# Splitting the last chunk of a start-up weight load over two DMA queues, and three more dummy matmuls beside it

## Chip, cores, metric

One core of one Trainium2 chip. The metric is the device time of one execution in microseconds (us). Beside it each run has a *span*: first to last instruction of the program, as the profiler records them.

## The reference

A conditioned transformer block on 2048 tokens of width 512: `mod = silu(c) @ w_mod` gives six vectors of 512; a layer norm is scaled and shifted by two of them, followed by attention with 32 query heads over the last 512 cached keys of 8 key heads, an output projection, a gated residual, and a second normalised and gated MLP.

```python
mod = (_silu(c) @ w_mod).reshape(c.shape[0], 6, 1, -1)
sa, ca, ga, sb, cb, gb = (mod[:, 0], mod[:, 1], mod[:, 2], mod[:, 3], mod[:, 4], mod[:, 5])
h = _layernorm(x, axis=-1) * (1 + ca) + sa
x = x + ga * _A_ref(h, A_k_cache, A_v_cache, A_wq, A_wo)
h = _layernorm(x, axis=-1) * (1 + cb) + sb
x = x + gb * _B_ref(h, B_w1, B_w2)
```

The first two slices of `w_mod` (for `sa` and `ca`) are needed before anything else, so their load stands at the very start.

## The kernel before

The loads at the start are issued from the sync engine (SP) and the scalar engine (ACT). Each chunk of `wm01` is 128 rows of 2 KB.

```python
    for i in range(2):
        dma(x_sb[:, 2 * i:2 * i + 2, :], ..., f"xa{i}", ..., eng=ACT if i else SP)
    dma(c_row[:, :], ...)
    for i in range(DC):                       # DC = 4
        load_wm01(i, (ACT, SP)[i % 2])
    for i, eng in enumerate((SP, SP)):
        dma(wq_sb[:, 2 * i:2 * i + 2, 0:QA * Dh], ...)   # first query weights
    load_k(0); load_wq(2, 2); load_v(0)
```

TensorE meanwhile runs dummy matmuls, then 32 products of one column (eight per chunk), transposes, two more dummies and the rest of the transposes:

```python
    def warm(n, gate=(), bk=7):               # n dummies of 512 columns into a spare bank
        for i in range(n):
            mm(bank[bk], ones[:, :], ones[:, 0:1].to_broadcast([P, QB]), True, True, ...)
    ...
    fs = mod_cols_mm(0, QBK)                  # 4 chunks x 2 slices x 4 columns
    for f in fs:
        f()
    ln_tposes(0, TB[0])
    mod_cols_evac(0, QBK)
    ... # cut
    ln_tposes(1, TB[0])
    warm(2, bk=1)
    ln_norm(2)
    mod_half(0, 0, DVE)
    mod_half(0, 2, ACT)
    ln_tposes(2, TB[1])
    ln_tposes(3, TB[1])
```

The kernel holds a second, general program as a fallback for odd values. A flag decides near the end, and here the fallback never runs. On TensorE it stands *after* the normal ending, so TensorE's last act is a jump over it:

```python
                if name == "pe":
                    with e.If(v == 128):
                        last_part()
                    with e.Else():
                        rerun()               # emits the general program; never runs here
```

## Time and profile before

| | before |
|---|---|
| time, 3 runs at first | 560.16 us (560.13 to 560.22) |
| span of the profiled run | 559.0 us (that run's time: 560.87) |
| TensorE busy | 553.9 us, 99% of the span |
| last chunk of the modulation weights lands | 8.82 us |
| first score matmul | 11.65 us |

TensorE is the bound from 11.65 us on.

### The profile page before, as it was taken

What the parts mean: (1) busy time and instruction counts of PE and PEld (TensorE: products, weight loads), DVE (VectorE), ACT (ScalarE), POOL (GpSimd) and SP (SyncE); (2) the same over time, 40 slices, a digit from 0 to 9 for tenths busy, and PEclk for the clock granted to TensorE, in tenths of its full rate; (3) what the DMA queues carried; (4) which work ended last, traced back from release to release, by engine and by line L of the source; (5) the groups of instructions that cost most, each with busy time, mean ns of one, the idle gap of its engine ahead of it and who ended that gap; (6) DMA issues with size and microseconds to landing.
All of it is one profiled execution on the core that took longest, in us unless ns stands there. A gap on an engine that the chain in (4) does not pass through costs nothing.

```text
span 559.0 us, 9759 instructions
## 1 busy us (share of the span) xinstructions
PE 553.9 (99%) x4139; PEld 316.6 (57%) x4139; DVE 254.9 (46%) x556; ACT 349.4 (63%) x455; POOL 52.7 (9%) x50
## 2 busy tenths in 40 slices
PE   8999999999999999999999999999999999999997
PEld 4665555555555555555555555555555554444444
DVE  5555555553546544335445443333354438322134
ACT  5986666666666666666666666666666644432500
POOL 2000022004400000033000000332000000000000
PEclk9999999999999999999999999999999999999999
DMA  9999763422224244353353312121123110200001
GB/s 234 296 196 185 136 166 42 114 43 73 38 41 74 39 84 106 61 130 58 96 95 57 76 40 39 39 38 38 39 39 76 39 29 0 50 28 21 21 29 48
DMA packets 113356, 42.66 MB, mean 76 GB/s; under 512 B 93976, under 2 KB 112152, under 8 KB 113304
## 3 DMA queue, kind: packets, MB, share of 16 engines
q1 hardware_dynamic: 112584, 41.08, 35.5%
q10 hardware_dynamic: 720, 0.89, 0.5%
q8 instruction: 33, 0.54, 0.4%
q14 instruction: 19, 0.16, 0.1%
HBM read 18.35 MB, written 2.10 MB: 37 GB/s over the span
## 4 chain that ended last, share of the span: by engine, by line
PE 98%; DMA 1%; SPq 0%; DVE 0%; issue 0%
PE psS L1374 29%; PE psO L1374 27%; PE psQ L1374 23%; PE psW L1374 20%; DMA wmw<-in_w_mod_dram 1%; SPq L1303 0%; PE psS L1377 0%; PE psO L1377 0%; DVE PT L1752 0%; DVE PT L1754 0%; PE psW L1377 0%
## 5 line engine op out<-in xcount | busy, mean ns | idle before, releaser
L1498 ACT ACTIVATE PT<-psS 128x1024 bf16<-128x1024 f32 x254 | 260.4, 1027 | 127.0 <-PE psS L1374 126.9
L1374 PE MATMUL psS<-qT,kT 128*128 128x512 bf16 (+1 forms) x516 | 151.8, 377 | 0.1
L1374 PEld LDWEIGHTS psO<-v,PT 128*128 128x128 bf16 x2048 | 126.6, 98 | 30.2
L1374 PE MATMUL psO<-v,PT 128*128 128x129 bf16 x2048 | 137.0, 220 | 0.0
L1374 PE MATMUL psW<-wo,oT 128*128 128x512 bf16 x512 | 130.6, 379 | 0.0
L1374 PE MATMUL psQ<-hT,wq 128*128 128x512 bf16 (+1 forms) x508 | 129.6, 377 | 0.0
L1508 DVE RECIPROCAL rinv<-psO 128x4 f32<-128x4 f32 x128 | 23.3, 182 | 225.3 <-PE psO L1374 225.3
L1509 DVE TENSOR_TENSOR o<-psO,rinv 128x512 bf16<-128x512 f32 x128 | 88.5, 691 | 4.7 <-DVE rinv L1508 0.3
L1374 PEld LDWEIGHTS psS<-qT,kT 128*128 128x128 bf16 x516 | 50.0, 98 | 58.7 <-issue 0.4
L1374 PEld LDWEIGHTS psQ<-hT,wq 128*128 128x128 bf16 x508 | 49.7, 98 | 59.0 <-ACT hT L1641 0.2
L1490 ACT ACTIVATE qT<-psQ 128x512 bf16<-128x512 f32 x125 | 73.9, 591 | 0.0
L1741 ACT ACTIVATE wq<-psS 128x512 bf16<-128x512 f32 x56 | 33.4, 597 | 49.1 <-PE psS L1374 49.1
L1374 PEld LDWEIGHTS psW<-wo,oT 128*128 128x128 bf16 x512 | 45.0, 98 | 32.9 <-DVE acc L1531 1.2
L1531 DVE TENSOR_TENSOR acc<-psW,acc 128x512 f32<-128x512 f32 x48 | 33.2, 691 | 6.7 <-PE psW L1374 6.7
L1374 PE MATMUL psO<-wmw,wq 128*128 128x512 bf16 (+1 forms) x168 | 32.9, 352 | 0.0
L1534 POOL TENSOR_TENSOR acc<-acc,gaf 128x512 f32<-128x512 f32 x12 | 15.6, 1301 | 146.9 <-DVE acc L1531 139.8
L1390 POOL TENSOR_TENSOR rstd<-rstd,cst 128x4 f32<-128x4 f32 x7 | 7.2, 1027 | 216.6 <-DVE rstd L1389 216.6
L1752 DVE TENSOR_TENSOR PT<-psO,gbf 128x512 f32<-128x512 f32 (+1 forms) x12 | 7.5, 624 | 40.4 <-PE psO L1374 40.4
L1374 PE MATMUL psS<-h2T,wmw 128*128 128x512 bf16 x112 | 25.3, 379 | 0.0
L1374 PEld LDWEIGHTS psO<-wmw,wq 128*128 128x128 bf16 x168 | 15.4, 98 | 16.5
L1374 PE MATMUL psS<-hT,wmw 128*128 128x512 bf16 x112 | 24.5, 379 | 0.0
L1384 DVE BATCH_NORM_STATS2 st<-x 128x6 f32<-128x512 bf16 x31 | 21.1, 680 | 3.7 <-DMA x<-in_A_x_dram 3.7
(93 smaller groups left out, 197.1 us busy)
## 6 DMA issues: line engine op xcount, KB each, us to landing
wo<-in_A_wo_dram SPq DMA_DIRECT2D x4, 1024.0 KB, 5.9
wq<-in_A_wq_dram SPq DMA_DIRECT2D x7, 512.0 KB, 4.5
wmw<-in_B_w_dram SPq DMA_DIRECT2D x14, 256.0 KB, 3.1
wmw<-in_w_mod_dram SPq DMA_DIRECT2D x4, 512.0 KB, 5.0
oT<-o SPq DMA_TRANSPOSE x128, 2.4
out_dram<-PT SPq DMA_DIRECT2D x15, 128.0 KB, 1.7
x<-in_A_x_dram SPq DMA_DIRECT2D x3, 512.0 KB, 4.3
v<-in_A_v_cache_dram SPq DMA_DIRECT2D x8, 128.0 KB, 4.5
```

The source lines that it names most:

```text
L1374: kb.op(PE, lambda e: e.matmul(out_ap, lhsT, rhs, start=start, stop=stop), reads=reads, group_writes=[R_b[k] for k in bk], signal=signal)
L1384: kb.op(DVE, lambda e: e.bn_stats(st[:, t, :], x_sb[:, t, :]), reads=[R_x[t]], writes=[R_st[t]])
L1390: kb.op(POOL, lambda e: e.tensor_tensor(rstd[:, sl], rstd[:, sl], cst[:, 0:1].to_broadcast([P, hi - lo]), op=ALU.pow), reads=R_rstd[sl] + ...
L1490: kb.op(ACT, lambda e: e.activation(qT[u % NQT][:, :], bank[bk], ACTF.Copy), reads=[R_b[bk]], writes=[R_qT[u % NQT]])
L1498: kb.op(ACT, lambda e: e.activation(PT[u % NPT][:, pr * 2:pr * 2 + 2, :], s_ps[pr][:, :, :], ACTF.Exp, scale=scale), reads=[R_b[pr * 2], R ...
L1508: kb.op(DVE, lambda e: e.reciprocal(rinv[:, u, :], o_ps[:, :, P]), reads=[R_b[5], R_b[6]], writes=[R_rinv])
L1509: kb.op(DVE, lambda e: e.tensor_tensor(o_sb[u % NOS][:, :, :], o_ps[:, :, 0:P], rinv[:, u, :].unsqueeze(2).to_broadcast([P, TPB, P]), op=A ...
L1531: kb.op(DVE, lambda e: e.tensor_tensor(acc[:, tl, :], bank[WBK], acc[:, tl, :], op=ALU.add), reads=[R_b[WBK], R_acc[tl]], writes=[R_acc[tl]])
L1534: kb.op(eng, lambda e: e.tensor_tensor(acc[:, tl, :], acc[:, tl, :], gaf[:, :], op=ALU.mult), reads=[R_acc[tl], R_ga], writes=[R_acc[tl]])
L1741: kb.op(ACT, lambda e: e.activation(h1T[b % 2][:, fc, :], bank[bk], ACTF.Relu), reads=[R_b[bk]], writes=[R_h1[b % 2][fc]], pre=all_events( ...
L1752: kb.op(DVE, lambda e: e.tensor_tensor(yt[i][:, c0:c1], bank[bk][:, c0:c1], gbf[:, c0:c1], op=ALU.mult), reads=[R_b[bk], R_gb], writes=[R_ ...
```

## The change

Its intent: let the last chunk come over both queues at once, and keep TensorE at work in the gaps so that its clock stays up.

```diff
-    R_wmc = RL("wmc", DC)
+    R_wmc = RL("wmc", DC + 1)
@@
     def load_wm01(i, eng=None):
-        dma(wm01[:, i, :], wm01v[:, i, :], f"wmc{i}", writes=[R_wmc[i]], eng=eng)
+        if i < DC - 1:
+            dma(wm01[:, i, :], wm01v[:, i, :], f"wmc{i}", writes=[R_wmc[i]], eng=eng)
+        else:
+            for sl, eng in enumerate((ACT, SP)):
+                dma(wm01[:, i, sl * D:(sl + 1) * D], wm01v[:, i, sl * D:(sl + 1) * D], f"wmc{i + sl}", writes=[R_wmc[i + sl]], eng=eng)
 
     def wm_res(sl, cc):
-        return R_wmc[cc] if sl < 2 else R_wm[sl]
+        return R_wmc[cc + (sl if cc == DC - 1 else 0)] if sl < 2 else R_wm[sl]
@@
-    for f in fs:
+    for i, f in enumerate(fs):
         f()
+        if i in (7, 23):
+            warm(1, bk=6)
@@
     ln_tposes(1, TB[0])
-    warm(2, bk=1)
+    warm(3, bk=1)
```

## The prediction

> **What bounds the kernel now.** I read the page first: busy shares, then the chain that ended last.
>
> ```profile
> PE 553.9 (99%) x4139; PEld 316.6 (57%) x4139; DVE 254.9 (46%) x556; ACT 349.4 (63%) x455; POOL 52.7 (9%) x50
> ...
> PE 98%; DMA 1%; SPq 0%; DVE 0%; issue 0%
> ```
>
> TensorE (PE) is busy for 99% of a span of 559.0 us, and 98% of the chain lies on it. The only other entry is 1% of DMA, the load of the first modulation weights, `wmw<-in_w_mod_dram`. Whatever the change does must therefore happen in the start, before PE runs without a break. So I asked for the chain by time over the first 12 us (columns: start us, length us, what).
>
> ```profile
> 2.05 6.77 DMA wmw<-in_w_mod_dram
> 8.82 0.05 issue
> 8.87 0.35 PE psQ L1374 x8
> 9.22 0.47 PE psS L1377 x8
> 9.69 0.43 PE psS L1374 x2
> 10.12 0.11 PE psO L1377 x2
> ...
> 10.57 0.52 PE psQ L1374 x4
> 11.09 0.44 PE psO L1374 x4
> 11.52 0.13 issue
> 11.65 0.38 PE psS L1374 x2
> ```
>
> The reader sees: the last chunk of the modulation weights, issued at 2.05 us, lands at 8.82; its eight one-column products (psQ), eight transposes, two dummies (psS L1374 x2), more transposes, then the first query products follow on PE with no real gap. From 11.65 on PE stays on the chain to the end. A delay or gain before that point reaches the end nearly one to one.
>
> The timeline of PE shows how the chunks come (start, length, what, idle before it and what ended it).
>
> ```profile
> 7.37 0.34 PE L1374 MATMUL psQ<-sc_bf,wmw 128*128 128x1 bf16 x8
> 8.11 0.55 PE L1374 MATMUL psQ<-sc_bf,wmw 128*128 128x1 bf16 x16 [0.40 <-DMA wmw<-in_w_mod_dram]
> 8.87 0.35 PE L1374 MATMUL psQ<-sc_bf,wmw 128*128 128x1 bf16 x8 [0.21 <-DMA wmw<-in_w_mod_dram]
> 9.08 0.61 PE L1377 MATMUL psS<-ident,xn 128*128 128x128 bf16 x8
> ```
>
> Two idle gaps, 0.40 and 0.21 us, each ended by a chunk's landing. The semaphore records of the trace give the landings: chunk 0 (ACT queue) 5.45, chunk 1 (SP) 8.06, chunk 2 (ACT) 8.24, chunk 3 (SP) 8.82. Each counts sixteen engine completions, and the last is an outlier: for chunk 3 fifteen are in by 7.93 and the sixteenth comes 0.89 us later. One slow DMA engine sets the time. The packet records show that engine alone from 7.5 us: a 2 KB packet about every 80 ns, first alternating between the two queues, then, after ACT's last packet ends at 7.84, the eight packets of chunk 3 back to back until 8.48; the semaphore follows 0.34 us later.
>
> VectorE (DVE) and ScalarE at the same place:
>
> ```profile
> 8.08 0.73 DVE L1395 TENSOR_SCALAR xn<-x,mv,rstd 128x512 bf16<-128x512 bf16 x2
> 9.26 0.17 DVE L1440 TENSOR_TENSOR modc<-psQ,m 128x8 f32<-128x8 f32 x1 [0.45 <-PE psQ L1374]
> 9.34 0.40 DVE L1395 TENSOR_SCALAR xn<-x,mv,rstd 128x512 bf16<-128x512 bf16 x1
> 9.73 0.73 DVE L1639 TENSOR_SCALAR hT<-psS,modc 128x256 bf16<-128x256 bf16 x2
> ```
>
> DVE idles 0.45 us before it copies out the products (modc), so at most about 0.45 us is to be won by an earlier landing: after that DVE's own normalisation, which ends at 8.81, is the bound.
>
> **What the Trainium skill says.** "DMA: Bandwidth & Descriptors", section "Issuing engines are not separate DMA queues": transfers issued from the scalar and the sync engine run on the same 16 DMA engines and interleave; a second issuer saves only sequencer time. The trace agrees: the slow engine alternates between the two queues at the same 80 ns a packet. The same page, "Queues, rings and completion order", says that each DMA engine goes round-robin between the queues it has work for, packet by packet; I use that to order the halves. "TensorE: Matmul & The Clock Gate", "Wait — 56ns, not 53.3ns?", gives 426.7 ns between 512-column matmuls cold and 215.7 warm. The trace agrees: the dummies start 427 ns apart until about 6.9 us, then the two at 9.53 and 9.74 are 216 ns apart. Its section "What's actually happening" puts the return to the cold clock after an idle window of about 3.4 us; the idle gaps here are 0.40 and 0.21 us, and no cold spacing returns in this trace.
>
> **The change, part by part.**
>
> (a) *The split.* Chunk 3 was one 256 KB DMA on the SP queue, 128 rows of 2 KB; it becomes two of 128 KB, rows of 1 KB, one on each queue. One issue more on ACT: about 0.45 us (its two wmw issues take 0.94), at 2.17, ahead of the table load. That load would end near 3.9 instead of 3.48, and ACT has nothing to do before x lands at 4.93: hidden. The queues were balanced before: ACT carried half of x and chunks 0 and 2, SP the other half and chunks 1 and 3, 768 KB each. After, ACT has 896 KB and SP 640 KB, with SP's next load, the first query weights (512 B rows), moving up behind its half. On the slow engine: the bytes are the same, but by the packet records' medians sixteen 1 KB packets take 16 x 46 = 0.74 us where eight of 2 KB take 8 x 84 = 0.67: +0.07. Round-robin then: SP's last packet of chunk 1 ends at 7.67, ACT has two of chunk 2 left (0.17). SP's half gets two in between, six of each side alternate to about 8.47, and ACT's last two share with two query-weight packets of 27 ns: 8.47 + 2 x 46 + 2 x 27 ns = 8.62, plus the 0.34 = 8.96. Against 8.82 that is +0.14; with better overlap of the small packets it is nearer +0.05. I take +0.10 us, on the path.
>
> (b) *Dummies after products 8 and 24.* Two 512-column matmuls on bank 6, 216 ns each at the warm rate. The first lies in the 0.40 us gap. The second follows chunk 2's products, whose last starts at 8.50, so it holds the array until about 8.74, and chunk 3 can start at 8.87 as before. Bank 6 has no reader yet, so no wait is added. Cost 0 as long as chunk 3 does not come earlier; else up to 0.2.
>
> (c) *Third dummy between the transposes.* Before, the two stream from 9.53 to 9.96, and the next transposes start exactly then: the dummies, not the data (the normalised tile was ready at 9.75), set that start. A third moves them to 10.18 and the first query product from 10.41 to 10.62. The four products of that group started at 10.41, 10.52, 10.62 and 10.80; the last waited for ScalarE's hT, ready at 10.75. Now, at 0.11 us each: 10.62, 10.73, 10.84, 10.95. So 0.15 of the 0.216 us stays on the path, through the copy of the query (11.12) to the first scores (11.65).
>
> Sum: +0.10 + 0 + 0.15 = +0.25 us; from 560.16 that is 560.4.
>
> **The rivals.**
>
> *R1: the split does bring the chunk earlier.* For it: fifteen of sixteen engines were done by 7.93, so another mix of packets may spare the slow engine its stall (one of its 2 KB packets may be the one of 746 ns at 6.07, which I cannot prove). Against: total bytes and engines are the same, and 2 KB and 1 KB rows differ little. Worth at most 0.45 us by DVE's idle time, less 0.15 for (c) and up to 0.2 for the second dummy: 559.7 to 560.1.
>
> *R2: the dummies mend the clock.* For it: that is evidently their aim, and nothing but them keeps PE busy between chunks. Against: the spacing is already 216 ns at 9.53 and stays there, and three runs agree within 0.09 us; there is nothing left to mend. Then (b) and (c) are worth zero or less. The opposite, a relapse to the cold clock for one window, would cost about half of 3.4 us, an estimate from the page's window: 561.9. I give it 2%.
>
> *R3: the load is hidden anyway*, because the landing is replaced by another wait at the same place: the query weights, landed at 9.22 and 9.74, are needed only from 10.41, and the keys, landed at 10.30, from 11.65. They have 0.6 us or more of slack, so I do not expect them to show. Then the result would be (c) alone: 560.3.
>
> **Range and chances.** Everything moves inside a stretch of 3 us out of 560; 2% would be 11.2 us, which no step here can reach. My middle is 560.35, between the sum and R1's pull downward. The range runs from R1's best, with the dummies hidden, to the sum with a slow engine delayed a further 0.5 us: 559.6 to 560.9. Faster by over 2%: 0.005; within 2%: 0.99; slower: 0.005.
>
> **What would show it right or wrong.** In the changed profile: (a) a third wmw issue on the ACT queue near 2.2 us, and the last eight products starting at 8.9 to 9.0 instead of 8.87; at 8.6 or earlier R1 holds. (b) One psO matmul in each gap, the idle gaps shorter by about 0.2 us and the products no later. (c) Three psS dummies 216 ns apart, the next transposes 0.2 us later relative to the last product, the first scores about 0.25 us later than 11.65. From there on the two traces should run parallel to the end. The prediction fails if the slow DMA engine is gone or slower still, or if the spacing falls back to 427 ns anywhere after 7 us.

## The result, and the profile after

| | time, us | span, us | time minus span, mean |
|---|---|---|---|
| before, same series, 6 runs | 560.23 (560.13 to 560.43) | 559.0 in the profiled run | 1.9 in the profiled run |
| change, 6 runs | 561.82 (561.33 to 562.19) | 558.3 to 559.0, mean 558.6 | 3.17 |

The ratio is 1.0027 (95% interval 1.0014 to 1.0040). I had said 560.35, between 559.6 and 560.9; the result lies outside. By the 2% class it is "same", but the six runs do not overlap with before's.

Now the profile. The page of the change opens with the same span to the tenth, and with almost the same busy times:

```profile
span 559.0 us, 9766 instructions
## 1 busy us (share of the span) xinstructions
PE 554.3 (99%) x4142; PEld 316.5 (57%) x4142; DVE 255.1 (46%) x556; ACT 349.6 (63%) x455; POOL 52.7 (9%) x50
```

Three more matmuls, three more weight loads, one more DMA issue: seven instructions, and no microsecond lost inside the span. The chain by time over the first 12 us (start, length, what):

```profile
2.20 6.44 DMA wmw<-in_w_mod_dram
8.64 0.05 issue
8.68 0.35 PE psQ L1378 x8
9.04 0.47 PE psS L1381 x8
9.51 0.65 PE psS L1378 x3
10.15 0.11 PE psO L1381 x2
...
10.64 0.56 ACT hT L1647
11.20 0.28 ACT qT L1627
11.49 0.14 issue
11.62 0.38 PE psS L1378 x2
```

In this trace the last half chunk, now ACT's, lands at 8.64 (before: 8.82). The three dummies hold TensorE for 0.65 us instead of 0.43, and the first scores start at 11.62 (before: 11.65). The dummies in the gaps are where they were meant to be:

```profile
7.12 0.35 PE L1378 MATMUL psQ<-sc_bf,wmw 128*128 128x1 bf16 x8
7.33 0.38 PE L1378 MATMUL psO<-ones 128*128 128x512 bf16 x1
7.77 0.59 PE L1378 MATMUL psQ<-sc_bf,wmw 128*128 128x1 bf16 x16
8.22 0.38 PE L1378 MATMUL psO<-ones 128*128 128x512 bf16 x1
8.68 0.35 PE L1378 MATMUL psQ<-sc_bf,wmw 128*128 128x1 bf16 x8
```

The extra issue on ACT pushes the table load to 2.69, as expected, and ACT still waits for x afterwards:

```profile
1.23 1.42 ACTq L1303 DMA_DIRECT2D wmw<-in_w_mod_dram  x3
2.69 1.28 ACT L1587 ACT_TABLE_LOAD   x1 [2.69 <-issue]
...
4.87 0.63 ACT L1589 ACTIVATE xn<-x 128x512 bf16<-128x512 bf16 x1 [0.68 <-DMA x<-in_A_x_dram]
```

From there the two traces run parallel: the last matmul ends at 555.80 before and at 555.77 after. So the loss is outside the span. The trace also holds what happens there, as semaphore updates without instructions. After the last instruction come a first group of nine updates of semaphore 2, then about 250 semaphores cleared in five ranges of some 50 side by side, then a second group of nine:

| us from the span's start | before | change |
|---|---|---|
| first group | 559.20 to 559.74 | 559.24 to 559.78 |
| semaphores 3 to 53 cleared, last | 560.31 | 560.35 |
| other four ranges cleared, last | 560.18 | 560.23 |
| second group | 560.53 to 560.89 | **561.96 to 562.32** |
| that run's time | 560.87 | 562.14 |

Up to the last clear the two agree within 0.05 us. Then the change waits 1.6 us where before waits 0.2, and the second group's end is the run's time within 0.2 us in both.

What does it wait for? The DMA view of the last microseconds of the change:

```profile
q8 instruction: 2, 0.03, 2.1%
q14 instruction: 1, 0.01, 0.4%
```

These are fetches of instructions. Queue 8 moves packets of 16,384 bytes, 33 in all: 0.54 MB, about the size of TensorE's 8284 recorded instructions (4142 matmuls and as many weight loads) at 64 bytes. The last one lands at 560.52 in the change, and the second group starts 1.44 us later. The Trainium skill, "Runtime: NRT & Kernel Launch", section "Instruction fetch mechanics", says that an engine's instructions are streamed in blocks of 16 KiB (256 instructions), that crossing a boundary is "mostly hidden", and that a taken branch breaks the prefetch. The same page, "The ~15µs preamble/postamble breakdown", lists a barrier, 51 semaphore resets per engine and another barrier after the kernel. The updates above look like that.

**Theory P (placement).** TensorE jumps over the fallback at the very end and fetches the block of its target. The closing code follows. The change lengthens TensorE's program by six instructions: TensorE's built program has 914,240 bytes instead of 913,856, which is 6 x 64. So the closing code lies 384 bytes further on, and a block boundary now falls ahead of the second barrier. TensorE gets there before the next block can be used.
**Theory A:** ScalarE's extra instruction, or the extra semaphore, lengthens the closing part.
**Theory C:** the start itself is slower in runs without a profile (a lost clock, another order of the DMAs).

### The profile page after: what moved, and what is told of

The parts are those of the page before. It is cut to its first block, busy times and chain, and to the rows that moved or that the text cites. A ratio compares the mean times of both kernels' runs of the same rounds, so it can differ in the third digit from the quotient of the medians. Undisturbed runs are those within 1.5% of the kernel's fastest.

```text
span 559.0 us, 9766 instructions
## 1 busy us (share of the span) xinstructions
PE 554.3 (99%) x4142; PEld 316.5 (57%) x4142; DVE 255.1 (46%) x556; ACT 349.6 (63%) x455; POOL 52.7 (9%) x50
## 4 chain that ended last, share of the span: by engine, by line
PE 98%; DMA 1%; ACTq 0%; ACT 0%; DVE 0%; issue 0%
PE psS L1378 29%; PE psO L1378 27%; PE psQ L1378 22%; PE psW L1378 20%; DMA wmw<-in_w_mod_dram 1%; ACTq L1303 0%; ACT hT L1647 0%; PE psS L1381 0%; PE psO L1381 0%; DVE PT L1758 0%; DVE PT L1760 0%; ACT qT L1627 0%; PE psW L1381 0%
```

## The experiments

For most of them I lengthen TensorE's program in the fallback, which never runs. Every executed instruction stays the same and only addresses move:

```diff
+        for _ in range(K // 2):      # a matmul is a weight load and a matmul: two instructions
+            PE.ops.append((lambda e: e.matmul(ps[0][0:1, 0:1], ones[:, 0:1], ones[:, 0:1], start=True, stop=True), [], []))
         SP.ops.append((lambda e: e.nop(), final_waits, []))     # end of the general program
```

I first tried no-operations there, but the build drops them. All sixteen runs below gave the reference's result. Below, *gap* is the time from the end of the first group to the start of the second in the profiled run, and *tail* the mean of time minus span. Before has gap 0.80 and tail 1.77 to 1.85.

### before_pad6: K = 6, before's instructions at the change's addresses

> The kernel before plus six TensorE instructions in the fallback program, which never runs: every executed instruction is the same, only TensorE's closing code lies 384 bytes further on, as in the change. Theory P (the time is lost after the last instruction, because TensorE's closing code now crosses a boundary of its instruction fetch): time 561.3 to 562.0, span as before, last closing semaphore update about 1.4 us later. Theory A (ScalarE's extra DMA issue or the extra semaphore lengthens the closing part) and theory C (the start itself became slower in runs without a profile): 560.2, same as before.

561.13 us (560.94 to 561.35) against 560.14 for before in the same rounds; gap 1.86, tail 2.92; the spans are *shorter* than before's if anything (558.0 to 558.5). Not one executed instruction differs, and 1.1 us are lost after the last. The loss is a matter of placement. (I had said 561.3 to 562.0: the direction is right, the size a little short.)

### change_pad250: the change with K = 250, so 256 instructions over before

> The change plus 250 TensorE instructions in the fallback program that never runs, so that TensorE's program is 256 instructions (16384 bytes) longer than before's and its closing code lies at the same place in a 16 KB block. Theory P: 560.0 to 560.4, the loss of 1.6 us gone. Theories A and C: 561.8 as the change.

560.50 us (559.93 to 561.17), gap 0.80, tail 1.80. With the closing code moved on to 256 instructions over before's, its old place within a 16 KB block by theory P, the loss of the change is gone. (The time is a little above my 560.0 to 560.4.) Theory A falls: ScalarE's instruction and the semaphore are still there.

### split_only: the diff without the three dummies

```diff
# against the change
-    for i, f in enumerate(fs):
+    for f in fs:
         f()
-        if i in (7, 23):
-            warm(1, bk=6)
-    warm(3, bk=1)
+    warm(2, bk=1)
```

> The split without any of the three dummies. TensorE's program has before's length, ScalarE's is one instruction longer, one semaphore more. Theory P: 559.9 to 560.3 (landing 0.2 us earlier as in the change's trace, no third dummy). Theory A: 561.3 to 562.0. Theory C with the DMA order at fault: 561.5 or more.

Gap 0.80, tail 1.81, so on the closing part P is right and A wrong once more. But the time is 561.61 (559.99 to 562.17), and this time it is lost *inside* the span: three of six runs have spans of 560.3 to 560.4 and a mean granted clock of 0.996 to 0.997. The profiled run is one of them. Two stretches of it (start:end and length in us; then the busy time and number of instructions of TensorE, its weight loads, VectorE, ScalarE and GpSimd; then the granted clock, the DMA share and GB/s):

```profile
6.43:9.85 3.42, 2.30 (x45) 1.59 (x43) 2.43 (x11) 1.39 (x4) 2.05 (x4) 1.00 1.26 195
9.85:13.26 3.41, 3.41 (x22) 2.32 (x20) 2.00 (x6) 1.96 (x4) 0.00 (x0) 0.50 1.19 287
```

For one window of 3.41 us the clock is at half, right after a window with little TensorE work. The timeline shows the cost:

```profile
9.19 0.35 PE L1378 MATMUL psQ<-sc_bf,wmw 128*128 128x1 bf16 x8 [0.37 <-DMA wmw<-in_w_mod_dram]
...
11.54 1.06 PE L1378 MATMUL psQ<-hT,wq 128*128 128x256 bf16 x4
12.40 1.03 PE L1378 MATMUL psO<-hT,wq 128*128 128x256 bf16 x4
13.25 0.61 PE L1378 MATMUL psS<-qT,kT 128*128 128x256 bf16 x4
```

Four query products take 1.03 us instead of 0.60, and the first scores start at 13.25. So Theory C is wrong for the change, whose traced starts are sound, but it names a real thing: this is what the dummies are for.

### dummies_only: the three dummies without the split

```diff
# against before; R_wmc, load_wm01 and wm_res stay as they were
+        if i in (7, 23):
+            warm(1, bk=6)
-    warm(2, bk=1)
+    warm(3, bk=1)
```

> The three dummies without the split. TensorE's program is six instructions longer, ScalarE's as before. Theory P: 561.5 to 562.0 (the closing 1.4 us plus about 0.15 for the third dummy), span up by about 0.15. Theory A: 560.4. Theory C: between 560.2 and 560.6.

561.63 us (561.20 to 562.26), gap 2.13, tail 3.05, mean span 558.6. ScalarE's program is as before, TensorE's is six instructions longer, and the loss is there: P.

### before_pad2, before_pad4, before_pad30, before_pad64: step or slope

> Two TensorE instructions more in the fallback that never runs (128 bytes). Theory P: the loss is a step, not a slope: either the closing gap between the two groups of closing updates is 0.8 us (time 560.1) or about 2 us (time 561.3), nothing between; with two instructions I expect 0.8 and 560.1. Rival S (each added instruction costs the same, 1.2 us over six): 560.5.

> Four more (256 bytes). Theory P: again 0.8 or about 2 us, whichever side of the step it is on. Rival S: 560.9.

> Thirty more (1920 bytes): the boundary then falls in the middle of TensorE's 51 closing semaphore clears. Theory P: its clears come in two bursts, split by the fetch, and the closing gap is 2.0 to 2.6 us (time 561.3 to 561.9). Rival S: 565 or more.

> Sixty-four more (4096 bytes): TensorE's program then ends beyond the boundary, so its closing code lies whole in the block that its last jump fetches anyway. Theory P: closing gap 0.8 us or less, time 560.1, in spite of ten times the added instructions. Rival S: 570 or more, or at least no less than with thirty.

Times 560.25, 561.22, 560.32 and 560.26 us against 560.18; tails 1.81, 2.91, 1.84, 1.83. It is a step, and the rival with a cost per instruction is dead: 64 instructions more cost nothing. With four the second group starts on time (gap 0.80) but needs 0.89 us instead of 0.36: the wait is now inside it, which my "0.8 or about 2 us, nothing between" had not foreseen. (One of its four runs, 564.2, also lost the clock window.) My own expectation for thirty was wrong: no two bursts, no loss, gap 0.86. The losing placements are a window, and I did not know its width.

### third_pad254, gaps_pad252, split_gaps_pad252, change_pad250b: the parts inside the span

All are padded to 256 instructions over before, so that the closing code is out of the way.

```diff
# third_pad254:       before, with warm(3, bk=1) for warm(2, bk=1);            K = 254
# gaps_pad252:        before, with the "if i in (7, 23): warm(1, bk=6)";       K = 252
# split_gaps_pad252:  the change, with warm(2, bk=1) for warm(3, bk=1);        K = 252
# change_pad250b:     the change;                                              K = 250
```

> Only the third dummy between the transposes, with TensorE's program padded to 256 instructions over before's, so that the closing code lies as before. My step (c): span 0.15 us over before's, time 560.3. If the third dummy is hidden: 560.1 to 560.2. Closing gap 0.8 us.

> Only the two dummies in the gaps between the chunks' products, padded likewise. My step (b): no cost, 560.1 to 560.2, and no run with the clock window lost (granted clock 0.996 or 0.997, 562.1). If the second dummy delays the last chunk's products: 560.3 to 560.4.

> The split and the two gap dummies, without the third, padded likewise: the best version by the parts if the split gains the 0.1 to 0.2 us that the change's trace shows at the landing. Then 559.9 to 560.2 and no lost clock window. If the split brings nothing in the mean: 560.2 to 560.6, as wide as the change with padding.

> The padded change a second time, in the same rounds as its parts: 560.2 to 560.7 (560.50 the first time), closing gap 0.8 us. Its difference to split_gaps_pad252 is the third dummy: 0.15 us by my step (c).

| kernel | time, us | runs that lost the clock window | mean span of the others | gap |
|---|---|---|---|---|
| before, same rounds | 560.35 (559.98 to 561.82) | 3 of 11 | 558.41 | – |
| third dummy only | 560.53 (560.30 to 561.81) | 1 of 6 | 558.72 | 0.80 |
| two gap dummies only | 560.33 (560.20 to 560.79) | 0 of 5 | 558.56 | 0.80 |
| split and gap dummies | 560.26 (560.22 to 560.48) | 0 of 5 | 558.50 | 0.80 |
| change, padded | 560.51 (560.19 to 560.84) | 0 of 6 | 558.63 | 0.80 |

The spans of one kernel scatter by 0.2 to 0.7 us, so differences of 0.1 between these means are not resolved. (The medians of the third dummy alone and of the gap dummies alone lie 0.1 to 0.2 us above what I had expected.) The third dummy alone can be had more sharply, from the traces. Where the last chunk's landing is the bound, I take the time from its first product to the first scores. Without the third dummy that is 2.78 (before: 8.87 to 11.65) and 2.79 us (before_pad18 below); with it 2.93 (third_pad254) and 2.94 (the change: 8.68 to 11.62). The two chains, first before_pad18, then third_pad254:

```profile
8.14 0.35 PE psQ L1376 x8
8.49 0.47 PE psS L1379 x8
8.97 0.43 PE psS L1376 x2
...
10.93 0.60 PE psS L1376 x4
```

```profile
8.68 0.35 PE psQ L1376 x8
9.03 0.47 PE psS L1379 x8
9.49 0.65 PE psS L1376 x3
...
10.63 0.56 ACT hT L1643
11.19 0.28 ACT qT L1625
11.48 0.14 issue
11.61 0.49 PE psS L1376 x3
```

So the third dummy costs 0.15 us on the path. The second gap dummy can hold the products: in gaps_pad252 chunk 3 had landed at 7.85, yet its products start only at 8.28, behind the dummy at 8.06.

```profile
7.66 0.54 PE L1376 MATMUL psQ<-sc_bf,wmw 128*128 128x1 bf16 x16
8.06 0.38 PE L1376 MATMUL psO<-ones 128*128 128x512 bf16 x1
8.28 0.34 PE L1376 MATMUL psQ<-sc_bf,wmw 128*128 128x1 bf16 x8
```

(The first dummy delays the products of chunks 1 and 2 there in the same way.) But the 0.22 us of the second do not reach the scores, because with so early a landing another chain is the bound: x, its statistics and its normalisation on VectorE, for which the transposes wait. In before_pad12, where chunk 3 lands at 7.52, the chain shows it:

```profile
0.79 3.76 DMA x<-in_A_x_dram
...
7.97 0.33 DVE xn L1397
8.30 0.05 issue
8.35 0.72 PE psS L1379 x8
...
11.03 0.60 PE psS L1376 x4
```

VectorE's second normalisation ends at 8.62 there, the transposes that read it start at 8.67, and the first scores follow 2.41 us after its end. The same 2.41 or 2.42 us are found with K = 2, 4, 6, 24 and 64, and in gaps_pad252 with its dummies (8.82 to 11.24). So in six of ten traces of before's own start the last chunk was not the bound at all, and a still earlier landing would have gained nothing.

The split's own effect stays open. Over ten traces of before's own start (before and its padded versions) the last chunk lands anywhere from 7.52 to 8.82 us; over five traces with the split the last half lands from 7.96 to 9.14. A tenth of a microsecond cannot be seen in that, and it would count only in the runs that the landing bounds. The best candidate, the split with the gap dummies, is at 0.9993 of before (95% interval 0.9979 to 1.0008): steadier in these runs, not shown to be faster.

### before_pad8, before_pad12, before_pad18, before_pad24: where does the wait sit?

> Eight TensorE instructions in the fallback. If the loss is a wait at the place where TensorE's closing code crosses into its next instruction block (theory P), two instructions earlier than with six: closing gap about 2 us, time 561.2. If only exactly four to six instructions lose (something else that the placement touches), gap 0.8 and 560.2.

> Twelve. Theory P: about 2 us again; if the crossing has by then moved into TensorE's semaphore clears, one of the five ranges of clears ends 1 to 1.4 us later than the other four, which names TensorE's range.

> Eighteen. Theory P in its first form (the crossing moves through the clears): one range of clears in two bursts, gap about 2 us. As thirty showed no loss, the other form is that the window of losing placements has ended: gap 0.8 to 0.9.

> Twenty-four, next to thirty, which lost nothing. Gap 0.8 to 0.9 and time 560.2 if the window ended before; about 2 us if it ends between 24 and 30.

Two runs each. Times 562.93, 563.05, 560.14 and 560.30 us against 560.10. Put in order of K, with the other placements, the wait walks backwards through the closing sequence (us from each span's start; "fetch" is the landing of the last 16,384-byte packet on queue 8):

| K | first group ends | fetch lands | clears of 3 to 53 end | second group | time minus span | the wait sits |
|---|---|---|---|---|---|---|
| 0 | 559.74 | 560.44 | 560.31 | 560.53 to 560.89 | 1.77 to 1.85 | nowhere |
| 2 | 559.13 | 559.61 | 559.71 | 559.93 to 560.29 | 1.81 | nowhere |
| 4 | 559.34 | 559.64 | 559.91 | 560.14 to 561.03 | 2.91 | within the second group |
| 6 | 559.24 | 559.55 | 559.82 | 561.10 to 561.46 | 2.92 | before the second group |
| 8 | 561.13 | 561.78 | 563.57 | 563.80 to 564.15 | 3.58 | before these clears (the other ranges ended by 561.53) |
| 12 | 562.00 | 559.90 | 562.57 | 562.80 to 563.15 | 1.75 | before the first group, inside the span |
| 18 | 559.05 | 559.68 | 559.63 | 559.85 to 560.21 | 1.84 | nowhere |
| 24 | 559.36 | 559.86 | 559.94 | 560.16 to 560.52 | 1.90 | nowhere |

With K = 8 the one range 3 to 53 is cleared 2 us after the other four, so that range belongs to the engine that waits (I had expected this for K = 12). With K = 12 the wait has moved in front of the program's last barrier, whose instruction on TensorE starts at 561.35 instead of about 558.3, and so it shows in the span:

```profile
core 0: 561.4 us, clock 0.997
```

(The 0.997 is the half clock while TensorE stands still at the end; this start lost no window. The profiled run with K = 8 did lose one, hence its late times; its second run, 561.89 with a span of 558.3, did not.) In these losing traces the engine goes on 1.4 to 1.6 us after the fetch has landed: 1.44 in the change, 1.55 with K = 6, 1.46 with K = 8, 1.45 with K = 12. The fetch itself keeps its schedule: in all eighteen traces, losing or not, it starts 2.12 to 2.16 us after the fetch before it has landed. What K moves is the instruction that needs the block. The size of the loss also follows the fetch: it took 1.22 us in the change and 0.95 with K = 6, most of the difference between their gaps (2.18 and 1.86). And at K = 18 nothing waits any more; by theory P the boundary then lies ahead of the place that the jump goes to, and all of the closing code is in that block. That last step is inferred from the pattern; the walk is measured.

One more rival can be settled from the traces: in each of them the granted clock falls to half at some point after the last matmul. With K = 18 it falls at 557.39, before the closing part, and nothing is lost; with K = 6 it falls only at 560.46, when the wait (559.82 to 561.10) is already under way. So the clock is not the cause.

So the losing placements begin at three or four instructions over before's length and end between 12 and 18: some 9 to 15 places. The change's six hit that window. Two things about it are not shown. That it recurs every 256 instructions is only argued: 256 over did not lose, but neither did 18 to 64, and no losing place one block further on was run. Nor is the place of the boundary derived: the built program of 913,856 bytes is 55 blocks and 199 instructions long, which by itself would put the next boundary 57 instructions on. Where the loaded program starts in its block no trace shows.

## Why the prediction was wrong, point by point

- **The bound and the place of action**: right for TensorE and for the span; in the two traces nothing after the first scores differs inside it. That the landing bounds the start held in the trace read, but in six of ten such traces VectorE's normalisation does. The prediction had named it as the next bound.
- **(a) the split, +0.10**: not confirmed and not refuted. The products of the last chunk started at 8.68, between its sign for the term (8.9 to 9.0) and R1's (8.6 or earlier). The working hung on one slow DMA engine in one trace. The landing moves by over a microsecond from run to run, so one trace could not carry a term of 0.1 us.
- **(b) gap dummies, 0**: right. When chunk 3 comes early, the second one does hold its products by 0.22 us, as the caveat there said, but in gaps_pad252 that stayed off the path.
- **(c) third dummy, +0.15**: right in size, 0.15 us. Its end, the copy of the query (qT), is right too, but with the third dummy the chain reaches it over ScalarE's hT and not over the query products.
- **The sum, +0.25 us**: in keeping with the span, in part by luck, as (a) is unconfirmed and the landing is often not the bound. Over twelve runs of the padded change the mean span is 558.68 against 558.41 for before's undisturbed runs, +0.27. Its median times are 560.50 and 560.51, and the 95% intervals of both ratios include 1.
- **The step that failed** is the last one: "from 560.16 that is 560.4". It adds a change of the span to the time, as though the 1.8 to 1.9 us between the two were a constant. The term was missing altogether. Its size is 1.3 to 1.4 us (tail 3.17 against 1.77 to 1.85), and it comes from where six added instructions put TensorE's closing code, not from what they do. before_pad6 shows it with nothing else changed (1.1 us there). With the span's +0.27 that makes up the measured +1.59 (560.23 to 561.82).
- **R2, "there is nothing left to mend"**: wrong, though not the cause of the miss. Three runs were too few. Of 62 runs with before's own start (32 of before, 30 of its padded versions) 6 lost one clock window at a cost of 1.3 to 2.6 us of span; split_only lost it in 3 of 6 and the third dummy alone in 1 of 6; with the gap dummies, in 0 of 34. That speaks for the gap dummies. It is no proof, as the rates differ between chips and builds.

## What to carry to other kernels

When a change adds or removes a handful of instructions and the time moves by a microsecond while the span does not, compare time minus span before explaining anything inside, then pad a part of the program that never runs: if the time comes back with the span unchanged, it was the placement. A gain of a tenth in the start cannot be judged from one trace, as the landing of a DMA there moves by more than that. And dummy matmuls that "do nothing" in the trace at hand may be guarding against a state that shows in one run of ten.

## What the Trainium skill lacked or had wrong

- "Runtime: NRT & Kernel Launch", "Instruction fetch mechanics": a crossing is called mostly hidden. In the closing code, soon after a taken jump, it was not, if theory P has the cause: the losing placements cost from 1.1 us (K = 4, by time minus span) to 2.95 us (K = 12: 563.05 against 560.10), and the engine went on only 1.4 to 1.6 us after the fetch had landed. The page warns of a taken branch's target, but not that a kernel's time can depend on where the code after it lies.
- The same page, "The ~15µs preamble/postamble breakdown": the parts are as listed, but the five ranges are cleared at the same time here, within 0.55 us in all (559.76 to 560.31 in before), where the page gives about 1.5 us for that stage. Whole closing part after the span: 1.9 us, or 3.3 us with the wait.
- "TensorE: Matmul & The Clock Gate", "What's actually happening": the return to the half clock is put to an idle window. Here the clock was lost after windows with TensorE busy for 2.30 of 3.42 us (split_only) and 2.66 of 3.42 us (before_pad8), and kept after 2.82 (before) and 3.21 (the change): not idle, only less busy; the longest single idle time there was 0.75 and 0.45 us. But it was also kept after 2.54 of 3.42 (split_gaps_pad252, 3.78 to 7.20), so this share does not tell the two outcomes apart. It counts each matmul's whole record and gives no threshold. (A later section of the page, "A second HAM failure mode: psum-queue depth-cycling", does put such a loss to short, frequent idle times.)
- No page says how far a load's landing moves from run to run: 7.52 to 8.82 us for the same 256 KB chunk in ten traces of the same start.
